# Attention kernel on one core: scores issued for six blocks at a time instead of four

## The chip, the cores and the metric

The kernel runs on one core of one Trainium2 chip. The metric is the device time of one execution in microseconds. Three runs of the kernel before took 1965.5, 1963.23 and 1964.68 us; the median is 1964.68 us.

## The reference

Two attention layers over the same input are mixed by a gate. Layer A has 32 query heads over one shared key and value head, layer B 32 full heads; a head has 16 columns, and there are 2048 tokens.

```python
def _A_ref(x, wq, wk, wv, wo):
    B, S, D = x.shape          # 1, 2048, 512
    H = 32; Dh = D // H        # 16
    q = (x @ wq).reshape(B, S, H, Dh).transpose(0, 2, 1, 3)
    k = x @ wk
    v = x @ wv
    p = softmax(einsum("bhqd,bkd->bhqk", q, k) * (Dh ** -0.5), axis=-1)
    o = einsum("bhqk,bkd->bhqd", p, v)
    return o.transpose(0, 2, 1, 3).reshape(B, S, H * Dh) @ wo
...
g = sigmoid((A_x * gate_w).sum(-1, keepdims=True))
return g * _A_ref(A_x, A_wq, A_wk, A_wv, A_wo) + (1 - g) * _B_ref(A_x, B_wqkv, B_wo)
```

`_B_ref` is the same with keys and values for each head.

## The kernel before

**Blocks.** The work is cut into eight groups of eight heads: a, b, a, b and so on (`groups`), each in two halves of 1024 queries. One *block* is 128 keys against 512 queries of one head, and there are 4096 of them in the list `blocks`. Two neighbouring blocks (two heads, a *pair*) have their scores made by two matmuls side by side on 64 rows each of TensorE (L490, `scores`), into one of three `sc` buffers in PSUM of two banks each. One exp on ScalarE over 128x1024 values (L494) reads the buffer and writes a `pr` buffer in SBUF; there are 2048 exps. Four blocks make a *quad*: its V product (L509, `values`) is four matmuls in f32 side by side on 32 columns each, shown as eight in the profile because each goes over TensorE twice. Sixteen quads add up in one auxiliary bank (`aux0` or `aux1`); then VectorE copies the bank out (`raw`, L514), DMAs sort the rows into `oT` and `dT`, and *norm* tasks (L425 to L432) divide.

**Projections.** Queries and keys of the next half or group, V of the next b group and the output projections are made while the exps run. They are cut into *units*, and a unit into *products* of TensorE (L172, each four matmuls side by side on 32 columns): 12 products for 512 tokens of queries or keys, 12 for four tiles of V, 3 for an output tile. A unit adds up in the auxiliary bank that the V products don't use at the time, and VectorE reads that bank when the unit is done (L333 queries and keys, L385 V, L410 and L412 output). So the next unit's first product waits for that read. The *lays* (L316) then move a finished projection's rows to their places by 32 DMAs from SyncE's queue, eight in each of four lays.

**The order around the change.** The whole order is written out by the program before it runs; each engine then executes its own list in order. One *step* is four blocks: `scores` for two pairs, `values` for the quad of two steps earlier, and `_Tasks.step`. This planner looks at the units still open and at their due steps, works out how many products a step are needed, and issues up to two; a unit's first product comes at the earliest a step after the last unit's end (`rest`). It also takes one side task (a norm, a weight's statistics) a step, and one lay every third step. `left` is the number of steps until the auxiliary banks change roles; a unit is opened only if it can end by then.

The main loop, and what the planner does in it, is in the functions printed here with the line numbers of the profile.

Of the kernel before, what the change touches and what calls it, by code (L numbers as in the profile page):

```python
# [23 lines left out]
NT = S // P  # L24
# [1 line left out]
NG = 4  # L26
BLK = 512
ACT = 2
STEP = 4
COLS = 32  # L30
SCALE = DH ** -0.5

# [3 lines left out]
UP = 2048.0  # L36
# [25 lines left out]
class _Tasks:  # L62
# [1 line left out]


    def __init__(self):
        self.now, self.credit, self.rest = 0, 0.0, 0
        self.units, self.open, self.side = [], deque(), deque()
        self.moves, self.moved = deque(), 0

    def add(self, units, after, due):
        self.units += [(after, due, u) for u in units]
# [8 lines left out]
    def _run(self, left):  # L81
        if not self.open:
            for u in self.units:
                if u[0] <= self.now and self.rest <= self.now and len(u[2]) <= 2 * (left - 1):
                    self.units.remove(u)
                    self.open.extend(u[2])
                    break
        if not self.open:
            return False
        self.open.popleft()()  # L90
        if not self.open:
            self.rest = self.now + 1
        return True

    def step(self, left):
        self.now += 1
        if self.side and self.side[0][0] <= self.now and len(self.open) not in (1, 2):
            self.side.popleft()[1]()
        if self.moves and self.moved <= self.now - 3:
            self.moved = self.now  # L100
            self.moves.popleft()()
        n = len(self.open)
        rate = n / max(1, left - 1)
        for u in self.units:
            n += len(u[2]) + 1
            rate = max(rate, n / max(1, u[1] - self.now))
        self.credit = min(self.credit + rate, 2.2)
        while self.credit >= 1.0 and self._run(left):
            self.credit -= 1.0

    def finish(self):
        while self.open:
            self.open.popleft()()
        self.rest = self.now + 1

    def flush(self):

        assert not self.moves
        self.rest = 0
        ahead = 0  # L120
        while self.open or self.units or self.side:
            if self.side and ahead < 2 and not (self.units and not ahead):
                self.side.popleft()[1]()
                ahead += 1
                continue
            ahead -= ahead > 0
            self.now += 100
            self._run(1 << 20)
            self.finish()
            self.rest = 0  # L130


def _sigmoid(nc, gate, z, scale):
# [8 lines left out]
def _fast(ctx, tc, x, wq_a, wk_a, wv_a, wo_a, wqkv_b, wo_b, gate_w, out, flag):  # L142
    nc = tc.nc
    cst = ctx.enter_context(tc.tile_pool(name="cst", bufs=1))
    inp = ctx.enter_context(tc.tile_pool(name="inp", bufs=8))
    wts = ctx.enter_context(tc.tile_pool(name="wts", bufs=2))
    ops = ctx.enter_context(tc.tile_pool(name="ops", bufs=2))
    prob = ctx.enter_context(tc.tile_pool(name="prob", bufs=6))
    ps_s = ctx.enter_context(tc.tile_pool(name="ps_s", bufs=3, space=PSUM))
    ps_x = ctx.enter_context(tc.tile_pool(name="ps_x", bufs=1, space=PSUM))  # L150

# [11 lines left out]
    vB = cst.tile([P, NT, 4, 3, DH], F32, name="vB")  # L163
# [31 lines left out]
    def load_w(src, gi, queues=(nc.sync, nc.sync)):  # L195

        cols = slice(gi * P, (gi + 1) * P)
        halves = []

        def one(part, at, bufs):  # L200
            w = inp.tile([P, BLK], F32, tag="in", name=f"w{part}{src}{gi}")
            w3 = w.rearrange("p (c m) -> p c m", c=NK)
            queues[part == "o"].dma_start(w if part == "o" else w3,
                                          at if part == "o" else at.rearrange("(c p) m -> p c m", p=P))
            w16 = wts.tile([P, 2, BLK], F16, tag=f"w{part}", name=f"w16{part}{src}{gi}", bufs=bufs)
            weights[src, gi, part] = w16

            def halve():
                split_weight(w16[:, 0], w16[:, 1], w)
                ready.add((part, src, gi))  # L210
                todo.add_side([lambda: absmax(f"w{part}_{src}", gi, w)], todo.now + 2)
# [49 lines left out]
    def x_unit(t):  # L261
        return [lambda: x_one(t, aux[1 - turn[0]])]
# [106 lines left out]
    def v_units(gi):  # L369
        w, state = weights["b", gi, "v"], {}  # L370

        def product(t, part):
            assert ("v", "b", gi) in ready
            a, b = PARTS[part]
            if t % 4 == 0 and part == 0:
                state["ps"] = aux[1 - turn[0]].rearrange("p (t a b d) -> p t a b d", t=4, a=4, b=2)
            ps = state["ps"]
            for c in range(NK):
                by_tiles(ps[:, t % 4].rearrange("p a b d -> p (a b d)"),
                         xT[:, a, c, t * P : (t + 1) * P], w[:, b, c * P : (c + 1) * P],  # L380
                         part == 0 and c == 0, part == 2 and c == NK - 1)
            if t % 4 < 3 or part < 2:
                return
            for hh in range(2):
                nc.vector.tensor_scalar(vB[:, t - 3 : t + 1, :, 2 * hh, :], ps[:, :, :, hh, :], UP ** -2, None,  # L385
                                        op0=ALU.mult)
# [5 lines left out]
        return [[lambda t=t, n=n: product(t, n) for t in range(b, b + 4) for n in range(3)]  # L392
                for b in range(0, NT, 4)]

    oT, dT, o16s = {}, {}, {}

# [21 lines left out]
    def norm_task(src, gi, half, t8, last):  # L418
        def norm():
# [13 lines left out]
            todo.add([o_unit(src, gi, 8 * half + t8, o16, last)], todo.now + 4,  # L433
                     todo.now + (32 if last and half else 52))

        return norm

# [31 lines left out]
    todo.add_side([gates], 15)  # L469


    groups = [(src, gi) for gi in range(NG) for src in "ab"]
# [23 lines left out]
    def values(m):  # L496
# [33 lines left out]
        todo.add_side([norm_task(src, gi, half, t8, last) for t8 in done8], todo.now + (3 if last and half else 7))  # L530

    def flag_stats():
        absmax("v_a", 0, vA[:, :, :DH], AX.XY)
# [28 lines left out]
    def begin(n, half):  # L562

        src, gi = groups[n]
        now = todo.now
        start = lambda n, half: (512 * n + 256 * half) // STEP
        sync = (nc.sync,)
        if half == 0:
            todo.add(q_units(src, gi, 1, sync), now if n else 12, start(n, 1) - 11)
        if n == 0 and half == 0:  # L570
            todo.add_side(load_w(*groups[1]), now + 6)
        if n + 2 < len(groups) and half:
            todo.add_side(load_w(*groups[n + 2]), now + 6)
        if n + 1 == len(groups):
            if half:
                todo.add_side([flag_stats], now + 12)
                todo.add_side([flag_reduce], now + 15)
                todo.add_side([flag_check], now + 27)
            return
        nxt = groups[n + 1]  # L580
        due = start(n + 1, 0) - 18
        if half == 0:
            if nxt[0] == "b":
                todo.add(k_units(nxt[1], 0, sync) + k_units(nxt[1], 1, sync), now + 22, due - 45)
                todo.add(v_units(nxt[1]), now + 22, due + 10)
        else:
            todo.add(q_units(*nxt, 0, sync), now + 3, due)

    turn[0] = 1
    steps = len(blocks) // STEP
    for j in range(steps + 2):
        if j < steps:
            if blocks[STEP * j][2:] == (0, 0, 0, 0, 0):
                begin(*blocks[STEP * j][:2])
            for u in range(STEP * j // ACT, STEP * (j + 1) // ACT):
                scores(u)
        if j >= 2:
            values(j - 2)  # L600
        for f in early.get(j, ()):
            f()
        todo.step(-(j - 1) % NT if j >= 2 else NT)
    todo.flush()


# [138 lines left out]
```

## Time and profile before

| what | before |
|---|---|
| median of three runs | 1964.68 us |
| the profiled execution's own time | 1963.35 us |
| its span | 1961.6 us |
| mean granted clock of TensorE | 0.994 |
| TensorE, matmuls busy | 1908.4 us (97%) |
| ScalarE busy | 1906.1 us (97%) |
| VectorE busy | 559.5 us (29%) |
| V products (L509), 8192 matmuls | 546.3 us for a, 545.5 us for b |
| scores (L490), 4096 matmuls | 319.8 us for a, 359.8 us for b |

A group's row on the page gives line, engine, operation, tiles out and in, shape and count, then the busy time, the mean duration of one, and the idle time of the engine just before them with what ended it. A row of the time line gives start in us, duration in us, engine, line, operation and count; neighbours of one kind are merged, and their overlapping durations are merged too, so the time between two starts says more of TensorE than a duration does.

### The profile page before, as it was taken

What the parts mean: (1) busy time and instruction counts of PE and PEld (TensorE: products, weight loads), DVE (VectorE), ACT (ScalarE), POOL (GpSimd) and SP (SyncE); (2) the same over time, 40 slices, a digit from 0 to 9 for tenths busy, and PEclk for the clock granted to TensorE, in tenths of its full rate; (3) what the DMA queues carried; (4) which work ended last, traced back from release to release, by engine and by line L of the source; (5) the groups of instructions that cost most, each with busy time, mean ns of one, the idle gap of its engine ahead of it and who ended that gap; (6) DMA issues with size and microseconds to landing.
All of it is one profiled execution on the core that took longest, in us unless ns stands there. A gap on an engine that the chain in (4) does not pass through costs nothing.

```text
span 1961.6 us, 46364 instructions
## 1 busy us (share of the span) xinstructions
PE 1908.4 (97%) x19472; PEld 517.5 (26%) x19472; DVE 559.5 (29%) x1093; ACT 1906.1 (97%) x2071; POOL 92.7 (5%) x103
## 2 busy tenths in 40 slices
PE   7999999999999999999999999999999999999997
PEld 4222322222222232222222233222222223222221
DVE  4225042141322414123142332412314241241414
ACT  4999999999999999999999999999999999999995
POOL 5001000200000100020000100002000000000000
PEclk8999999999999999999999999999999999999998
DMA  4022100101011110110101210011100111001012
GB/s 142 7 48 50 31 12 15 47 12 33 7 33 47 33 27 7 31 36 11 29 12 31 59 33 14 12 33 28 27 19 17 34 41 32 12 12 28 6 29 82
DMA packets 55416, 59.82 MB, mean 30 GB/s; under 512 B 21440, under 2 KB 29632, under 8 KB 55200
## 3 DMA queue, kind: packets, MB, share of 16 engines
q1 hardware_dynamic: 53984, 55.66, 11.9%
q8 instruction: 155, 2.54, 0.6%
q0 software_dynamic: 528, 0.69, 0.1%
q14 instruction: 61, 0.50, 0.1%
q10 hardware_dynamic: 688, 0.43, 0.1%
HBM read 10.55 MB, written 4.19 MB: 8 GB/s over the span
## 4 chain that ended last, share of the span: by engine, by line
PE 63%; ACT 18%; issue 13%; DVE 5%; SPq 1%; DMA 0%; ACTq 0%; DVEq 0%
PE aux L509 32%; PE sc L490 19%; ACT pr L494 18%; PE aux L172 11%; DVE dTa L425 1%; DVE stats L176 1%; SPq L316 0%; DMA acc<-in_A_x_dram 0%; DVE lob L180 0%; DVE acc L412 0%; DVE xT L247 0%; SPq L525 0%; DVE yb L333 0%; DVE rawb L514 0%; PE aux L275 0%
## 5 line engine op out<-in xcount | busy, mean ns | idle before, releaser
L494 ACT ACTIVATE pr<-sc 128x1024 f32<-128x1024 f32 x2048 | 1895.2, 1261 | 10.5 <-PE sc L490 6.5
L509 PE MATMUL aux<-pr,vA 128*32 128x512 f32 x4096 | 546.3, 605 | 0.0
L509 PE MATMUL aux<-pr,vB 128*32 128x512 f32 x4096 | 545.5, 605 | 0.0
L490 PE MATMUL sc<-Qb,K 64*128 64x512 f16 x2048 | 359.8, 383 | 18.0
L490 PE MATMUL sc<-Qa,kA 64*128 64x512 f16 x2048 | 319.8, 382 | 3.7 <-ACT pr L494 0.2
L490 PEld LDWEIGHTS <-K 64*128 64x128 f16 x2048 | 99.8, 93 | 466.6 <-issue 464.0
L412 DVE SCALAR_TENSOR_TENSOR acc<-aux,gate_up,acc 128x512 f32<-128x512 f32 x112 | 84.0, 750 | 437.4 <-PE aux L172 437.4
L490 PEld LDWEIGHTS <-kA 64*128 64x128 f16 x2048 | 71.0, 94 | 258.4 <-issue 243.9
L509 PEld LDWEIGHTS aux<-pr,vA 128*32 128x32 f32 x4096 | 80.6, 108 | 197.4 <-issue 195.1
L509 PEld LDWEIGHTS aux<-pr,vB 128*32 128x32 f32 x4096 | 80.9, 108 | 128.5 <-issue 122.2
L172 PE MATMUL aux<-w16ob,o16b 128*32 128x512 f16 x768 | 69.2, 392 | 8.3 <-DVE acc L412 6.0
L172 PEld LDWEIGHTS <-xT 128*32 128x32 f16 x3072 | 55.5, 97 | 63.9 <-issue 63.9
L172 PE MATMUL aux<-xT,w16qb 128*32 128x512 f16 x768 | 66.2, 379 | 3.8 <-DVE rawb L514 2.2
L172 PE MATMUL aux<-w16oa,o16a 128*32 128x512 f16 x768 | 68.6, 379 | 0.1
L172 PE MATMUL aux<-xT,w16qa 128*32 128x512 f16 x768 | 65.8, 379 | 1.3 <-DVE ya L333 0.9
L385 DVE TENSOR_SCALAR vB<-aux 128x256 f32<-128x256 f32 x32 | 12.1, 420 | 181.9 <-PE aux L172 181.9
L425 DVE RECIPROCAL dTb<-dTb 128x128 f32<-128x128 f32 x64 | 60.5, 946 | 10.0 <-DMA dTb<-rawb 9.8
L425 DVE RECIPROCAL dTa<-dTa 128x128 f32<-128x128 f32 x64 | 60.5, 945 | 7.9 <-DMA dTa<-rawa 7.9
L172 PE MATMUL aux<-w16vb,xT 128*32 128x128 f16 x3072 | 61.8, 219 | 0.7 <-DVE rawa L514 0.7
L333 DVE TENSOR_SCALAR yk<-aux 128x512 f32<-128x512 f32 x16 | 11.1, 692 | 176.6 <-PE aux L172 176.6
L172 PE MATMUL aux<-xT,w16kb 128*32 128x512 f16 x768 | 60.9, 379 | 0.0
L333 DVE TENSOR_SCALAR ya<-aux 128x512 f32<-128x512 f32 x16 | 11.1, 692 | 170.6 <-PE aux L172 170.6
(119 smaller groups left out, 598.9 us busy)
## 6 DMA issues: line engine op xcount, KB each, us to landing
acc<-in_A_x_dram SPq DMA_DIRECT2D x16, 256.0 KB, 6.0
oTa<-rawa SPq DMA_DIRECT2D x128, 32.0 KB, 1.9
dTa<-rawa SPq DMA_DIRECT2D x128, 32.0 KB, 2.0
K<-hik SPq DMA_DIRECT2D x128, 32.0 KB, 1.9
K<-lok SPq DMA_DIRECT2D x128, 32.0 KB, 1.9
Qb<-hib SPq DMA_DIRECT2D x128, 32.0 KB, 1.9
Qb<-lob SPq DMA_DIRECT2D x128, 32.0 KB, 2.0
out_dram<-acc SPq DMA_DIRECT2D x16, 256.0 KB, 2.1
```

What stands on the lines that cost most here:

```text
L172: nc.tensor.matmul(out[n : n + COLS], lhsT[:, n : n + COLS], rhs, start=start, stop=stop)
L176: nc.vector.tensor_reduce(stats[:, n, i : i + 1], src, axis=axis, op=ALU.max, apply_absolute_value=True)
L333: nc.vector.tensor_scalar(y, state["ps"], UP ** -2, QK_MAX, op0=ALU.mult, op1=ALU.min)
L385: nc.vector.tensor_scalar(vB[:, t - 3 : t + 1, :, 2 * hh, :], ps[:, :, :, hh, :], UP ** -2, None, op0=ALU.mult)
L412: nc.vector.scalar_tensor_tensor(acc[:, t], state["ps"], g, acc[:, t], op0=ALU.mult, op1=ALU.add)
L425: nc.vector.reciprocal(d, d)
L490: nc.tensor.matmul(sc[:, i], k[r, c * P : (c + 1) * P], Q[src, gi, half, p][r, j * BLK : (j + 1) * BLK], start=True, stop=True)
L494: nc.scalar.activation(probs[u][:, :m], sc[:, :m], AF.Exp, scale=SCALE / (UP * UP))
L509: nc.tensor.matmul(o[32 * i : 32 * i + 32, :], v, probs[at // ACT][:, at % ACT], start=c == 0, stop=c == NT - 1)
```

## The change

The unit of the loop becomes a *burst* of six blocks. In a burst the scores of three pairs are issued one behind another, then the quads whose exps belong to earlier bursts: one in odd bursts, two in even ones. The planner no longer works with rates. It has a clock in nanoseconds with a price for each kind of work (product 216, V product 882, the three pairs 863, three exps 2712). Of three exps' time it takes off the scores and the V products, and issues products of units for what is left, ahead of, between and behind the V products; up to 1990 may be carried over. A new unit may open 880 after the last product of the one before. One side task is taken at each quad, one lay at each burst. V units have six products for two tiles instead of twelve for four. `prob` has seven buffers instead of six, `inp` seven instead of eight. All due times are converted from steps to bursts, some with other distances; the early transposes and key blocks are spread over eight bursts instead of eleven steps.

```diff
-STEP = 4
+BURST = 6
+PRODUCT = 216
+VALUES = 882
+SCORES = 863
+EXPS = 2712
+MOST = 1990
+EMPTY = 880
...
-                if u[0] <= self.now and self.rest <= self.now and len(u[2]) <= 2 * (left - 1):
+                if u[0] <= self.now and self.empty <= self.clock and len(u[2]) <= 1.5 * (left - 1):
...
         self.open.popleft()()
+        self.clock += PRODUCT
         if not self.open:
-            self.rest = self.now + 1
+            self.empty = self.clock + EMPTY
         return True

-    def step(self, left):
-        self.now += 1
+    def products(self, room, left):
+
+        if left <= 1:
+            self.finish()
+        while room >= PRODUCT and self._run(left):
+            room -= PRODUCT
+        return room
+
+    def beside(self):
         if self.side and self.side[0][0] <= self.now and len(self.open) not in (1, 2):
             self.side.popleft()[1]()
-        if self.moves and self.moved <= self.now - 3:
-            self.moved = self.now
-            self.moves.popleft()()
-        n = len(self.open)
-        rate = n / max(1, left - 1)
-        for u in self.units:
-            n += len(u[2]) + 1
-            rate = max(rate, n / max(1, u[1] - self.now))
-        self.credit = min(self.credit + rate, 2.2)
-        while self.credit >= 1.0 and self._run(left):
-            self.credit -= 1.0
...
-    inp = ctx.enter_context(tc.tile_pool(name="inp", bufs=8))
+    inp = ctx.enter_context(tc.tile_pool(name="inp", bufs=7))
...
-    prob = ctx.enter_context(tc.tile_pool(name="prob", bufs=6))
+    prob = ctx.enter_context(tc.tile_pool(name="prob", bufs=7))
...
-                nc.vector.tensor_scalar(vB[:, t - 3 : t + 1, :, 2 * hh, :], ps[:, :, :, hh, :], UP ** -2, None,
+                nc.vector.tensor_scalar(vB[:, t - 1 : t + 1, :, 2 * hh, :], ps[:, :2, :, hh, :], UP ** -2, None,
                                         op0=ALU.mult)
...
-    early = {0: p1, 1: t1, 2: x_unit(12), 3: x_unit(13), 4: x_unit(14), 5: p2, 6: t2, 7: x_unit(15), 8: p3, 10: t3}
+    early = {0: (p1, []), 1: (t1, x_unit(12)), 2: (x_unit(13), []), 3: (p2, []), 4: (t2, x_unit(14)),
+             5: (x_unit(15), []), 6: (p3, []), 7: (t3, [])}
...
-    steps = len(blocks) // STEP
-    for j in range(steps + 2):
-        if j < steps:
-            if blocks[STEP * j][2:] == (0, 0, 0, 0, 0):
-                begin(*blocks[STEP * j][:2])
-            for u in range(STEP * j // ACT, STEP * (j + 1) // ACT):
-                scores(u)
-        if j >= 2:
-            values(j - 2)
-        for f in early.get(j, ()):
-            f()
-        todo.step(-(j - 1) % NT if j >= 2 else NT)
+    done = spare = 0
+    for k in range(-(-len(blocks) // BURST) + 1):
+        todays = blocks[BURST * k : BURST * (k + 1)]
+        todo.now += 1
+        todo.clock = max(todo.clock, k * EXPS) + SCORES
+        for u in range(BURST // ACT * k, BURST // ACT * k + len(todays) // ACT):
+            if blocks[ACT * u][2:] == (0, 0, 0, 0, 0):
+                begin(*blocks[ACT * u][:2])
+            scores(u)
+        quads = min(BURST * k, len(blocks)) // 4 - done
+        spare = min(spare + EXPS - SCORES, MOST)
+        room = spare - VALUES * quads
+        front, behind = early.get(k, ((), ()))
+        for f in front:
+            f()
+        for m in range(done, done + quads):
+            room = todo.products(room, -m % NT)
+            values(m)
+            todo.clock += VALUES
+            todo.beside()
+        done += quads
+        spare = max(todo.products(room, -done % NT), 0)
+        for f in behind:
+            f()
+        if todo.moves:
+            todo.moves.popleft()()
     todo.flush()
```

In the lists of instructions below, `sc956` is the buffer use for pair 956, `pr954` the output of exp 954, `aux0` and `aux1` are the auxiliary banks, and `w16ob1` is an output weight. Each pair has two matmuls and each product four; one row of each is shown. TensorE before, in the middle of the kernel, two steps:

```order
L490 MATMUL sc956_11873<-Qb111_10723,K11_7655 128x512 [waits Activation_49]
...
L490 MATMUL sc957_11878<-Qb111_10723,K11_7655 128x512 [waits Activation_49]
...
L509 MATMUL aux0_82<-pr952_11840,vB_91 32x512 x2
L509 MATMUL aux0_82<-pr953_11845,vB_91 32x512 x2
...
L490 MATMUL sc958_11897<-Qb111_10723,K11_7655 128x512 [waits Activation_49]
...
L490 MATMUL sc959_11902<-Qb111_10723,K11_7655 128x512 [waits Activation_49]
...
L509 MATMUL aux0_82<-pr954_11858,vB_91 32x512 x2
L509 MATMUL aux0_82<-pr955_11863,vB_91 32x512 x2
```

TensorE now, at the same place, an odd and an even burst:

```order
L492 MATMUL sc957_11978<-Qb111_10938,K11_7622 128x512 [waits Activation_49]
...
L492 MATMUL sc958_11983<-Qb111_10938,K11_7622 128x512 [waits Activation_49]
...
L492 MATMUL sc959_11988<-Qb111_10938,K11_7622 128x512 [waits Activation_49]
...
L511 MATMUL aux0_82<-pr954_11945,vB_91 32x512 x2
L511 MATMUL aux0_82<-pr955_11950,vB_91 32x512 x2
L492 LDWEIGHTS K12_7660
L492 MATMUL sc960_12002<-Qb112_10983,K12_7660 128x512 [waits Activation_49]
...
L492 MATMUL sc962_12012<-Qb112_10983,K12_7660 128x512 [waits Activation_49]
...
L511 MATMUL aux0_82<-pr956_11955,vB_91 32x512 x2
L511 MATMUL aux0_82<-pr957_11981,vB_91 32x512 x2
L511 MATMUL aux0_82<-pr958_11986,vB_91 32x512 x2
L511 MATMUL aux0_82<-pr959_11991,vB_91 32x512 x2
```

Between two returns to the scores there stood one V product and now there stand one or two. Pair 959 uses the buffer of pair 956, and pair 962 that of pair 959: the last pair of a burst waits for the last exp of the burst before.

The second place is where one output unit ends and the next begins. TensorE before: the last product of a unit, two steps, and the first product of the next unit, which waits for VectorE's read of the bank:

```order
L172 MATMUL aux0_82<-w16ob1_5287,o16b10_11470 32x512
...
L490 MATMUL sc968_12008<-Qb112_10787,K12_7730 128x512 [waits Activation_49]
...
L509 MATMUL aux1_83<-pr964_11961,vB_91 32x512 x2
L509 MATMUL aux1_83<-pr965_11966,vB_91 32x512 x2
...
L490 MATMUL sc970_12022<-Qb112_10787,K12_7730 128x512 [waits Activation_49]
...
L509 MATMUL aux1_83<-pr966_11992,vB_91 32x512 x2
L509 MATMUL aux1_83<-pr967_11997,vB_91 32x512 x2
...
L172 MATMUL aux0_82<-w16ob1_5287,o16b10_11470 32x512 [waits DVE_49]
```

TensorE now, a few microseconds of work further on, in one burst:

```order
L492 MATMUL sc977_12163<-Qb112_10983,K12_7660 128x512 [waits Activation_49]
...
L173 MATMUL aux0_82<-w16ob1_5295,o16b10_11553 32x512
...
L511 MATMUL aux1_83<-pr972_12133,vB_91 32x512 x2
L511 MATMUL aux1_83<-pr973_12138,vB_91 32x512 x2
...
L173 MATMUL aux0_82<-w16ob1_5295,o16b10_11553 32x512 [waits DVE_49]
...
L492 MATMUL sc978_12190<-Qb112_10983,K12_7660 128x512 [waits Activation_49]
```

One V product now stands between the two units where two steps stood.

More of the change, by code (lines that the diff above doesn't have):

```diff
@@ L66, in __init__ @@
     def __init__(self):
-        self.now, self.credit, self.rest = 0, 0.0, 0
+        self.now, self.clock, self.empty = 0, 0, 0
         self.units, self.open, self.side = [], deque(), deque()
-        self.moves, self.moved = deque(), 0
+        self.moves = deque()
     def add(self, units, after, due):
@@ L127, in flush @@
             self.now += 100
+            self.clock += 10 * EMPTY
             self._run(1 << 20)
             self.finish()
-            self.rest = 0
 def _sigmoid(nc, gate, z, scale):
@@ L210, in halve @@
                 ready.add((part, src, gi))
-                todo.add_side([lambda: absmax(f"w{part}_{src}", gi, w)], todo.now + 2)
+                todo.add_side([lambda: absmax(f"w{part}_{src}", gi, w)], todo.now + 1)
             halves.append(halve)
@@ L374, in product @@
             a, b = PARTS[part]
-            if t % 4 == 0 and part == 0:
+            if t % 2 == 0 and part == 0:
                 state["ps"] = aux[1 - turn[0]].rearrange("p (t a b d) -> p t a b d", t=4, a=4, b=2)
@@ L390, in product @@
                     absmax("v_b", 4 * gi + b, vB[:, 4 * b : 4 * b + 4], AX.XYZW)
-        return [[lambda t=t, n=n: product(t, n) for t in range(b, b + 4) for n in range(3)]
-                for b in range(0, NT, 4)]
+        return [[lambda t=t, n=n: product(t, n) for t in range(b, b + 2) for n in range(3)]
+                for b in range(0, NT, 2)]
     oT, dT, o16s = {}, {}, {}
@@ L432, in norm @@
                 nc.vector.tensor_sub(o16[:, 1], o, o16[:, 0])
-            todo.add([o_unit(src, gi, 8 * half + t8, o16, last)], todo.now + 4,
-                     todo.now + (32 if last and half else 52))
+            todo.add([o_unit(src, gi, 8 * half + t8, o16, last)], todo.now + 3,
+                     todo.now + (21 if last and half else 35))
         return norm
@@ L467, in gates @@
         nc.vector.tensor_scalar(gate_up, gate_up, UP ** -2, None, op0=ALU.mult)
-    todo.add_side([gates], 15)
+    todo.add_side([gates], 10)
     groups = [(src, gi) for gi in range(NG) for src in "ab"]
@@ L529, in values @@
             done8 = range(4 * (s - 2), 4 * (s - 1)) if s >= 2 else []
-        todo.add_side([norm_task(src, gi, half, t8, last) for t8 in done8], todo.now + (3 if last and half else 7))
+        todo.add_side([norm_task(src, gi, half, t8, last) for t8 in done8], todo.now + (2 if last and half else 3))
     def flag_stats():
@@ L565, in begin @@
         now = todo.now
-        start = lambda n, half: (512 * n + 256 * half) // STEP
+        start = lambda n, half: (512 * n + 256 * half) // BURST
         sync = (nc.sync,)
         if half == 0:
-            todo.add(q_units(src, gi, 1, sync), now if n else 12, start(n, 1) - 11)
+            todo.add(q_units(src, gi, 1, sync), now if n else 9, start(n, 1) - 8)
         if n == 0 and half == 0:
-            todo.add_side(load_w(*groups[1]), now + 6)
+            todo.add_side(load_w(*groups[1]), now + 4)
@@ L572, in begin @@
         if n + 2 < len(groups) and half:
-            todo.add_side(load_w(*groups[n + 2]), now + 6)
+            todo.add_side(load_w(*groups[n + 2]), now + 4)
         if n + 1 == len(groups):
             if half:
-                todo.add_side([flag_stats], now + 12)
-                todo.add_side([flag_reduce], now + 15)
-                todo.add_side([flag_check], now + 27)
+                todo.add_side([flag_stats], now + 8)
+                todo.add_side([flag_reduce], now + 10)
+                todo.add_side([flag_check], now + 18)
@@ L579, in begin @@
             return
         nxt = groups[n + 1]
-        due = start(n + 1, 0) - 18
+        due = start(n + 1, 0) - 12
         if half == 0:
             if nxt[0] == "b":
-                todo.add(k_units(nxt[1], 0, sync) + k_units(nxt[1], 1, sync), now + 22, due - 45)
-                todo.add(v_units(nxt[1]), now + 22, due + 10)
+                todo.add(k_units(nxt[1], 0, sync) + k_units(nxt[1], 1, sync), now + (3 if n else 10), due - 30)
+                todo.add(v_units(nxt[1]), now + (3 if n else 10), due + 7)
@@ L586, in begin @@
         else:
-            todo.add(q_units(*nxt, 0, sync), now + 3, due)
+            todo.add(q_units(*nxt, 0, sync), now + 2, due)
     turn[0] = 1
-    steps = len(blocks) // STEP
-    for j in range(steps + 2):
-        if j < steps:
-            if blocks[STEP * j][2:] == (0, 0, 0, 0, 0):
-                begin(*blocks[STEP * j][:2])
-            for u in range(STEP * j // ACT, STEP * (j + 1) // ACT):
-                scores(u)
-        if j >= 2:
-            values(j - 2)
-        for f in early.get(j, ()):
-            f()
-        todo.step(-(j - 1) % NT if j >= 2 else NT)
+    done = spare = 0
```

8 lines of the change are left out of this document (3 added, 5 removed).

## The prediction

> **What bounds the kernel now.** I read the page's busy times first, then its groups, then the time line around single exps.
>
> ```profile
> PE 1908.4 (97%) x19472; PEld 517.5 (26%) x19472; DVE 559.5 (29%) x1093; ACT 1906.1 (97%) x2071; POOL 92.7 (5%) x103
> PE 63%; ACT 18%; issue 13%; DVE 5%; SPq 1%; DMA 0%; ACTq 0%; DVEq 0%
> L494 ACT ACTIVATE pr<-sc 128x1024 f32<-128x1024 f32 x2048 | 1895.2, 1261 | 10.5 <-PE sc L490 6.5
> ```
>
> TensorE and ScalarE both look full, and the chain of waits changes between them. So the question is which of the two has slack, and where. ScalarE's own pace must come first. The next two rows come from two windows of the time line with one beginning; the third column of numbers, after the x, is the count of exps merged.
>
> ```profile
> 404.37 17.08 ACT L494 ACTIVATE pr<-sc 128x1024 f32<-128x1024 f32 x18
> 404.37 116.99 ACT L494 ACTIVATE pr<-sc 128x1024 f32<-128x1024 f32 x127
> 28.28 1.04 ACT L494 ACTIVATE pr<-sc 128x1024 f32<-128x1024 f32 x1
> 1924.36 12.52 ACT L494 ACTIVATE pr<-sc 128x1024 f32<-128x1024 f32 x13
> ```
>
> Between the ends of exp 18 and exp 127 lie 99.91 us, so an exp takes **0.917 us** when nothing starves it. The first starts at 28.28 and the last ends at 1924.36 + 12.52 = 1936.88: 1908.6 us for 2048 exps. At full pace they would take 1.02 + 2047 x 0.9167 = 1877.5. So ScalarE loses only **31 us** in the whole kernel, and no version with these exps can gain more than that. Some 8 to 9 us are lost in the first stretch (from 28.28 to 52.72, the tenth step of two and so 18 exps later, by a row quoted further down: 24.4 us instead of 16.5). The other 22 us are lost where TensorE is too full:
>
> ```profile
> 1000.84 0.61 PE L172 MATMUL aux<-xT,w16qa 128*32 128x512 f16 x8
> 1001.39 0.61 PE L490 MATMUL sc<-Qa,kA 64*128 64x512 f16 x4
> 1001.92 1.06 PE L509 MATMUL aux<-pr,vA 128*32 128x512 f32 x8
> 1002.80 0.40 PE L172 MATMUL aux<-xT,w16qa 128*32 128x512 f16 x4
> 1003.14 0.61 PE L490 MATMUL sc<-Qa,kA 64*128 64x512 f16 x4
> 1939.48 0.83 PE L172 MATMUL aux<-w16ob,o16b 128*32 128x512 f16 x12 [0.84 <-DVE acc L412]
> 1940.36 0.75 DVE L412 SCALAR_TENSOR_TENSOR acc<-aux,gate_up,acc 128x512 f32<-128x512 f32 x1 [0.93 <-PE aux L172]
> 1941.16 0.83 PE L172 MATMUL aux<-w16ob,o16b 128*32 128x512 f16 x12 [0.85 <-DVE acc L412]
> ```
>
> Starts count here, since ends overlap. A V product (x8) holds TensorE 1002.80 - 1001.92 = 0.88. A projection product (x4) holds it 0.215: 0.83 for three against 0.40 for one. One product and the way back to the scores take 0.34, so this switch is 0.12. A step of two exps with one product lasts 1.75 (1001.39 to 1003.14), with two 1.97; ScalarE needs 1.83. So steps with two products starve ScalarE, and the rest does not.
>
> **What the change does to TensorE's load.** One switch out of the scores and one back served two exps, and now serve three. Per six exps (two bursts) TensorE has six score pairs, three V products and on average 3.3 projection products: 2 x (0.12 + 2 x 0.21 + 0.32) + 3 x 0.87 + 3.3 x 0.215 = 5.0 us, against 5.50 for the exps. Load is no longer the bound. (0.21 is a pair before another: 0.53 from the first pair to V, less 0.32, below.)
>
> The Trainium skill, "TensorEngine Tiling (Array Packing)", section Key Properties, states that a change of tiling mode drains the engine. The trace agrees (0.12 and about 0.10 beyond the matmuls themselves), and by this rule alone 341 fewer rounds save some 75 us of TensorE and the kernel gets faster; that is the first rival.
>
> **What it does to the order.** The scores tile has three buffers. The third pair of a burst needs the buffer of the exp just ahead of the burst, the last one that ScalarE was given. TensorE executes in order, so everything behind this pair waits for that exp. Then come all V and projection products of the burst, and only behind them the first pair of the next burst. The rows for the links of this chain:
>
> ```profile
> 56.41 1.03 ACT L494 ACTIVATE pr<-sc 128x1024 f32<-128x1024 f32 x1
> 57.49 0.09 PEld L490 LDWEIGHTS <-kA 64*128 64x128 f16 x1 [0.23 <-issue]
> 57.81 0.16 PEld L509 LDWEIGHTS aux<-pr,vA 128*32 128x32 f32 x8 [0.23 <-issue]
> 52.23 0.61 PE L490 MATMUL sc<-Qa,kA 64*128 64x512 f16 x4
> 52.72 1.02 ACT L494 ACTIVATE pr<-sc 128x1024 f32<-128x1024 f32 x1 [0.72 <-PE sc L490]
> ```
>
> An exp ends at 57.44, and the pair that waits for its buffer starts at 57.49: **0.05**. From that pair to the V product: **0.32**. Switch back: **0.12**. From a pair to its exp's start, ScalarE idle: 52.72 - 52.23 = **0.49**. A starved exp until its end: **1.02**. Together 2.00 us, plus W, the products of one burst. The chain starts at the end of the exp before the burst and ends with the first exp of the next burst, four exps later, for which ScalarE needs 4 x 0.917 = 3.67. So a burst starves nothing only if **W is at most 1.67 us**. Each microsecond above that is a loss, carried on two bursts later, because the burst after next waits for this late exp's followers.
>
> The same chain existed before, with one V product inside: W = 0.88 + 0.215 or 0.43, so 0.36 to 0.57 below the limit. Now a burst with two V products has 2 x 0.87 = 1.75 (0.85 to 0.88 each, since the 0.88 holds the switch from the scores) before any projection product. Those bursts are every second one. The listing of the changed order gives, for the 335 pairs of an even and an odd burst (after the first 12), projection products in the even / odd one: 0/5 in 96, 0/0 in 80, 1/4 in 65, 0/4 in 51, 1/1 or 1/2 in 28, 0/1 to 0/3 in 14, 3/0 in one. Excess over 1.67:
> - even, none: 0.08; even, one: 0.295; even, three: 0.72
> - odd, four: 0.88 + 0.86 = 1.74, so 0.07; odd, five: 1.955, so 0.28; fewer: none.
>
> The even bursts alone: 241 x 0.08 + 93 x 0.295 + 0.7 = **47 us**. If every pair costs the larger of its two: 96 x 0.28 + 93 x 0.295 + 145 x 0.08 + 0.7 = **67 us**. The even and the odd chain run side by side and whichever is late holds up the other through ScalarE, so the loss lies between: stepping "the end two bursts on is the later of this end + 3.83 + W and the next end + 2.75" through the list gives about 59. I take **58**.
>
> Evictions. A new unit's first product waits until VectorE has read the auxiliary bank. The rows at 1939.48 to 1941.16 show such units back to back: 1.68 us for three products of 0.645, so 1.03 us from the end of the last product to the next unit. The planner now leaves 0.88, before it left a whole step (1.75). About 195 units run under the exps (46 of queries and keys, 32 of V, some 120 of the output). 0.15 for two thirds of them is 20 us, and more where a norm (four VectorE operations, 1.78 us by the rows below) stands in front; half of it will fall on bursts that have room. Ends: 0, and 195 x 0.15 + 16 halves x 1.8 = 58. I take **20**, near the lower rows.
>
> Start. Three key blocks and four transposed tiles stand in eight bursts instead of eleven steps; the same work on the same engines. Between 5 and 12 us lost; I take 8, as before.
>
> ```profile
> 993.12 0.95 DVE L425 RECIPROCAL dTb<-dTb 128x128 f32<-128x128 f32 x1
> 994.90 0.95 DVE L425 RECIPROCAL dTb<-dTb 128x128 f32<-128x128 f32 x1
> ...
> L385 DVE TENSOR_SCALAR vB<-aux 128x256 f32<-128x256 f32 x32 | 12.1, 420 | 181.9 <-PE aux L172 181.9
> ...
> 31.73 1.22 SPq L316 DMA_DIRECT2D Qa<-hia  x2
> 33.00 1.22 SPq L316 DMA_DIRECT2D Qa<-loa  x2
> ```
>
> From norm to norm VectorE takes 1.78 us; a V unit's read is 0.42; SyncE issues two transfers in 1.27.
>
> Other edits cost nothing I can see. VectorE reads V in 64 pieces instead of 32; a 128x128 piece of this kind isn't in the trace, so it is bounded by nothing and the old 0.42 each, and VectorE is 29% busy; what of it TensorE waits for is in the evictions' bounds. The four lays of a projection now leave one a burst: 8 issues of 0.63 are 5.1 us against 2.75, so SyncE's queue runs up to 10 us behind, covered by due times 8 to 12 bursts (22 to 33 us) ahead; uncovered, scores would wait those 10 us at each of 23 projections. One buffer more for the exps' output, one less for weights: weights are loaded at least half a group (128 exps, some 117 us) ahead, which covers it.
>
> The sum: losses of 58 + 20 + 8 = 86 instead of 31, so +55 us. The profiled execution took 1963.35 us (span 1961.6; the median of the runs is 1.3 above it). 1963.35 + 55 = **2018 us**.
>
> **Rivals.**
> 1. *Faster: the third buffer doesn't matter.* If the third pair came free early enough, the exps would run at 0.917 throughout and only the start would cost: 31 - 8 = 23 us less, 1940 us. For it: TensorE's load, 5.0 against 5.5. Against it: 2.00 + 1.75 exceeds 3.67 with no projection product at all. It decides if the links are 0.3 shorter than my rows, so that W may be 1.97 and one product beside two V products fits; from 0.2 shorter on the kernel would already gain.
> 2. *No change.* Links 0.16 shorter (W up to 1.83) and free evictions: 93 x 0.135 + 96 x 0.125 + 0.6 = 25, with the start 33 instead of 31, so 1965 us. It needs both at once.
> 3. *Slower, but less.* The even chain alone, evictions hidden: 47 + 8 - 31 = +24, 1987 us.
> 4. *Much slower.* Units often meet norms on VectorE: 67 + 58 + 10 - 31 = +104, 2067 us.
>
> The Trainium skill, "Perfetto Trace Analysis", section Optimization Strategy, says that the same gap repeated on the engine that should be saturated can mean too little SBUF or PSUM for the next tile. The runs of before show hardly any such gap on ScalarE (10.5 us); by this page I would expect one at every second burst's first exp, at the forecast's time.
>
> That the change doesn't do what it says can be left out: the listing shows bursts of three pairs and one or two V products.
>
> **How the numbers follow.** Forecast 0.76, rival 3 0.10, rival 4 0.04, rival 2 0.03, rival 1 0.07. A measurement can tell about 0.2% from no change here. So slower 0.90, same 0.03, faster 0.07. The range leaves out rivals 1, 2 and 4 and little of 3: from 1985 (the even chain alone) to 2040 (67 + 35 + 8 - 31 = +79).
>
> **What would show it.** Right: the mean distance of exps rises from 0.932 (1908.6 / 2047) to about 0.959; ScalarE's idle time from 10.5 us to some tens, ended by the score line; the third pair of a burst starts 0.05 after an exp's end; the first exp of a burst starts late, most often behind bursts with two V products and one projection product, or one and five; TensorE waits for VectorE at output units for about 0.15. Wrong: exps at 0.917 from end to end in stretches with projection products, or a starved first exp without a third pair that waited.

## The result, and the profile after

The changed kernel takes 2025.87 us (median of four runs, 2024.77 to 2026.62), the kernel before 1963.95 us (1963.09 to 1965.5): 1.0314 times as long, 95% interval 1.0296 to 1.0332, or +61.9 us. The profiled execution took 2025.17 us at a clock of 0.994 as before; its span is 2023.4 us.

First the page of the changed kernel: busy times, the shares of the chain that ended last, then the groups of exps (L496) and scores (L492). Lines below the change have moved by one or two.

```profile
PE 1872.9 (93%) x19472; PEld 567.3 (28%) x19472; DVE 563.0 (28%) x1125; ACT 1925.3 (95%) x2071; POOL 93.1 (5%) x103
PE 60%; ACT 25%; issue 7%; DVE 6%; DMA 1%; SPq 0%; ACTq 0%; DVEq 0%; POOL 0%
L496 ACT ACTIVATE pr<-sc 128x1024 f32<-128x1024 f32 x2048 | 1914.1, 1038 | 53.2 <-PE sc L492 42.0
L492 PE MATMUL sc<-Qb,K 64*128 64x512 f16 x2048 | 338.0, 381 | 68.6 <-ACT pr L496 66.7
L492 PE MATMUL sc<-Qa,kA 64*128 64x512 f16 x2048 | 322.7, 381 | 37.5 <-ACT pr L496 32.9
```

TensorE has less to do (1872.9 us busy, 1908.4 before) and stands at 93% instead of 97%. Yet ScalarE is idle for 53.2 us instead of 10.5. The two score rows hold the answer: TensorE itself was idle 106 us ahead of scores, and 99.6 of it ended with an exp. So each engine waits for the other. The view of waits says the same (engine and line, what it waited for: us in total, times, longest). The first fence is the changed kernel, the second the kernel before, whose view has no row of scores that wait for an exp among its larger ones.

```profile
PE sc L492 <- ACT pr L496: 99.7, 309, 0.5
ACT pr L496 <- PE sc L492: 42.0, 105, 2.0
PE aux L173 <- DVE acc L413: 10.7, 10, 1.7
```
```profile
PE aux L172 <- DVE acc L412: 6.0, 7, 0.9
ACT pr L494 <- PE sc L490: 6.5, 12, 1.2
```

The first and the last exps of the changed kernel, from two windows of its time line:

```profile
29.45 1.04 ACT L496 ACTIVATE pr<-sc 128x1024 f32<-128x1024 f32 x1
1986.60 13.40 ACT L496 ACTIVATE pr<-sc 128x1024 f32<-128x1024 f32 x14 [1.97 <-PE sc L492]
```

From 29.45 to 1986.60 + 13.40 = 2000.00 are 1970.55 us, 62 more than the 1908.6 before. The whole change of time lies in this stretch: what lies around it is 52.9 us in sum, as before (53.0). At full pace 2048 exps need 1877.5, so 93 us are lost, where 31 were. About 7.5 of them fall on the first 48 exps; in the other 1999 the ends lie 0.9595 apart on average, which is 85.5 us over 0.9167 each.

Here is one turn of the chain, at an even burst with one projection product ahead of its two V products. The first fence has TensorE's rows of the time line, the second ScalarE's.

```profile
408.35 0.39 PE L492 MATMUL sc<-Qb,K 64*128 64x512 f16 x2 [0.52 <-ACT pr L496]
408.67 0.40 PE L173 MATMUL aux<-xT,w16qa 128*32 128x512 f16 x4
408.90 1.89 PE L511 MATMUL aux<-pr,vB 128*32 128x512 f32 x16
410.72 0.39 PE L492 MATMUL sc<-Qb,K 64*128 64x512 f16 x2
```
```profile
409.98 1.07 ACT L496 ACTIVATE pr<-sc 128x1024 f32<-128x1024 f32 x1
411.21 1.02 ACT L496 ACTIVATE pr<-sc 128x1024 f32<-128x1024 f32 x1 [0.17 <-PE sc L492]
```

TensorE stood for 0.52 us ahead of the third pair, until an exp let go of its buffer. Behind it come one product and sixteen matmuls of V, and only at 410.72 the first pair of the next burst: 2.37 us from pair to pair. ScalarE ended its last exp at 409.98 + 1.07 = 411.05 and got the next at 411.21. That one also lasts the full 1.02, with nothing to overlap, so it ends 0.27 late: the gap of 0.17 and 0.10 more. This is why ScalarE's idle time on the page (53.2) says less than the loss (85.5).

Then I went through every burst after the first 16: how many V and projection products it has by the order, and by how much the first exp of the *next* burst ends later than 0.917 after the one ahead of it.

| V / projection products in the burst | bursts | W by the prediction | over 1.67 | median lateness | sum |
|---|---|---|---|---|---|
| 1 / none to 3 | 123 | up to 1.53 | none | 0.00 | 0.1 us |
| 1 / 4 | 115 | 1.74 | 0.07 | 0.05 | 13.8 us |
| 1 / 5 | 95 | 1.955 | 0.28 | 0.24 | 29.9 us |
| 2 / none | 240 | 1.75 | 0.08 | 0.07 | 11.1 us |
| 2 / 1 | 92 | 1.965 | 0.295 | 0.27 | 30.7 us |
| 2 / 3 | 1 | 2.39 | 0.72 | 1.40 | 1.4 us |

Exps at the second and third place of a burst are never late. Of 399 first exps that come over 0.02 late, with 86.8 us together, 371 (83.5 us) follow a burst whose last pair started within 0.07 us of the end of the exp that held its buffer (a *held* pair). Held pairs are the rule here, 550 of these 666 bursts have one, so this count alone proves little. What tells is the work behind them: of 114 bursts with a held pair, one V product and at most three products, only one is followed by a late exp. In the kernel before there were 184 late ones with 23.5 us, and only 2.6 us of that behind a pair that was held.

### The profile page after: what moved, and what is told of

The parts are those of the page before. It is cut to its first block, busy times and chain, and to the rows that moved or that the text cites. A ratio compares the mean times of both kernels' runs of the same rounds, so it can differ in the third digit from the quotient of the medians.

```text
span 2023.4 us, 46408 instructions
## 1 busy us (share of the span) xinstructions
PE 1872.9 (93%) x19472; PEld 567.3 (28%) x19472; DVE 563.0 (28%) x1125; ACT 1925.3 (95%) x2071; POOL 93.1 (5%) x103
## 4 chain that ended last, share of the span: by engine, by line
PE 60%; ACT 25%; issue 7%; DVE 6%; DMA 1%; SPq 0%; ACTq 0%; DVEq 0%; POOL 0%
PE aux L511 27%; ACT pr L496 25%; PE sc L492 21%; PE aux L173 12%; DVE dTb L426 1%; DVE acc L413 1%; DVE dTa L426 1%; DMA acc<-in_A_x_dram 0%; DVE xT L248 0%; DVE oTb L427 0%; DVE o16b L433 0%; DVE oTa L427 0%; DVE stats L177 0%; DVE o16b L432 0%; ACT xT L247 0%
## 5 line engine op out<-in xcount | busy, mean ns | idle before, releaser
L496 ACT ACTIVATE pr<-sc 128x1024 f32<-128x1024 f32 x2048 | 1914.1, 1038 | 53.2 <-PE sc L492 42.0
L511 PE MATMUL aux<-pr,vB 128*32 128x512 f32 x4096 | 508.1, 597 | 0.0
L511 PE MATMUL aux<-pr,vA 128*32 128x512 f32 x4096 | 506.8, 596 | 0.0
L492 PE MATMUL sc<-Qb,K 64*128 64x512 f16 x2048 | 338.0, 381 | 68.6 <-ACT pr L496 66.7
L492 PE MATMUL sc<-Qa,kA 64*128 64x512 f16 x2048 | 322.7, 381 | 37.5 <-ACT pr L496 32.9
L492 PEld LDWEIGHTS <-K 64*128 64x128 f16 x2048 | 101.9, 94 | 456.1 <-issue 418.9
L492 PEld LDWEIGHTS <-kA 64*128 64x128 f16 x2048 | 100.0, 94 | 388.1 <-issue 336.3
L511 PEld LDWEIGHTS aux<-pr,vB 128*32 128x32 f32 x4096 | 108.9, 109 | 172.4 <-issue 148.2
L511 PEld LDWEIGHTS aux<-pr,vA 128*32 128x32 f32 x4096 | 109.0, 109 | 162.8 <-issue 136.7
L516 DVE COPY rawb<-aux 128x512 f32<-128x512 f32 x32 | 22.1, 692 | 343.6 <-PE aux L511 340.0
L426 DVE RECIPROCAL dTb<-dTb 128x128 f32<-128x128 f32 x64 | 60.5, 946 | 11.1 <-DMA dTb<-rawb 11.1
L334 DVE TENSOR_SCALAR yk<-aux 128x512 f32<-128x512 f32 x16 | 11.1, 691 | 185.6 <-PE aux L173 185.6
L386 DVE TENSOR_SCALAR vB<-aux 128x128 f32<-128x128 f32 x64 | 15.6, 286 | 155.7 <-PE aux L173 155.7
L173 PE MATMUL aux<-xT,w16qb 128*32 128x512 f16 x768 | 52.3, 382 | 3.3 <-DVE rawb L516 1.4
```

Of the source, the lines that this page charges most:

```text
L173: nc.tensor.matmul(out[n : n + COLS], lhsT[:, n : n + COLS], rhs, start=start, stop=stop)
L334: nc.vector.tensor_scalar(y, state["ps"], UP ** -2, QK_MAX, op0=ALU.mult, op1=ALU.min)
L386: nc.vector.tensor_scalar(vB[:, t - 1 : t + 1, :, 2 * hh, :], ps[:, :2, :, hh, :], UP ** -2, None, op0=ALU.mult)
L426: nc.vector.reciprocal(d, d)
L492: nc.tensor.matmul(sc[:, i], k[r, c * P : (c + 1) * P], Q[src, gi, half, p][r, j * BLK : (j + 1) * BLK], start=True, stop=True)
L496: nc.scalar.activation(probs[u][:, :m], sc[:, :m], AF.Exp, scale=SCALE / (UP * UP))
```

## The experiments

Theory 1 is the chain of the prediction: the third pair waits for an exp, and the work W behind it is too long. The rivals are that TensorE's load and its switches decide (theory 2; a switch is the way between scores and the other products), or that evictions (VectorE's reads of the auxiliary bank between units) make most of it (theory 3). For the first four the kernel before took 1962.96 us on their chip, 1.0 less than above, so their distances from the changed kernel's 2025.87 are good to about 1 us.

**1. The third pair behind the first V product.** The same products; only the place of the third pair moves, at the cost of one more round out of the scores and back wherever other work follows it.

```diff
         for u in range(BURST // ACT * k, BURST // ACT * k + len(todays) // ACT):
             if blocks[ACT * u][2:] == (0, 0, 0, 0, 0):
                 begin(*blocks[ACT * u][:2])
-            scores(u)
+            if u % 3 < 2 or not k:
+                scores(u)
...
             values(m)
+            if m == done and 3 * k + 2 < len(blocks) // ACT:
+                scores(3 * k + 2)
```

> The third pair of each burst is issued behind the burst's first V product instead of ahead of it; everything else as in the changed kernel. Theory 1 (the chain through the third buffer bounds the kernel): the products between this pair and the next burst fall from at most 1.96 us to at most 1.1 us, below the limit of 1.67, so the third pair hardly ever starves ScalarE any more; but each burst has one more way out of the scores and back (0.22), so TensorE itself becomes the bound in the dense stretches (2 x 0.86 of scores, 2.6 of V, 1.1 of projections and 0.44 for six exps: 5.85 against 5.50). Sum: about 2013 us, some 13 below the changed kernel, and the number of third pairs that start 0.05 us after an exp's end with a starved exp behind them falls to a few tens. Theory 2 (TensorE's own load bounds the changed kernel): 683 more rounds of 0.22 add 150 us, about 2170 us. Theory 3 (evictions bound it): no change within 5 us of 2026.

Measured: 2015.83 us (2015.02 to 2016.71), 1.0271 times before (1.0254 to 1.0288). Its waits, and the shares of its chain:

```profile
ACT pr L496 <- PE sc L492: 53.3, 150, 2.1
PE sc L492 <- ACT pr L496: 46.0, 97, 0.5
```
```profile
PE 73%; ACT 13%; issue 7%; DVE 5%; DMA 1%; SPq 0%; ACTq 0%; DVEq 0%; POOL 0%
```

The trace has 1148 rounds out of the scores and back where the changed kernel has 683: 465 more and not the 683 more of the expectation, because in the other bursts the third pair runs straight into the next burst's scores. At 0.22 each, theory 2 then gives about 2128 us. More switches, and yet 10 us less: load as the only cause falls. Scores now wait for exps half as long (46.0 us for 99.7). But what is left has another look: of 74.0 us of late exps only 9.1 follow a held pair, and the chain runs over TensorE for 73%. In 48.1 of the 74.0 us TensorE's rows show no gap above 0.06 us for more than 5 us ahead of the late exp's burst (19.8 of 87.0 us in the changed kernel). So the wait went, and most of what is lost now falls where TensorE is full; that the additional switches are what fills it is likely, but was not separated.

**2. The same products, but in the bursts with two V products.** Even bursts may take two products, odd ones three, whatever their time; nothing is carried over.

```diff
-        room = spare - VALUES * quads
+        room = (2 if quads > 1 else 3) * PRODUCT
...
-        spare = max(todo.products(room, -done % NT), 0)
+        todo.products(room, -done % NT)
```

> The same bursts and the same products, handed out otherwise: up to two in the bursts with two V products and up to three in those with one, instead of mostly none and four or five. TensorE's load is the same. Theory 1: bursts with two V products and two projection products hold 1.75 + 0.43 = 2.18 us between the third pair and the next burst, 0.51 over the limit; the listing has 218 of them, so 111 us, with 8 for the others and evictions as before: about 2073 us, 47 above the changed kernel. Theory 2 (load): no change, 2026 within 10. Theory 3 (evictions): the same number of units, no change within 10.

Measured: 2077.9 us, 1.0586 (1.0564 to 1.0607). From the page and the waits of this kernel:

```profile
PE 1866.2 (90%) x19472; PEld 553.9 (27%) x19472; DVE 563.3 (27%) x1125; ACT 1922.8 (93%) x2071; POOL 92.5 (4%) x103
```
```profile
PE sc L492 <- ACT pr L496: 166.4, 434, 0.5
ACT pr L496 <- PE sc L492: 108.2, 244, 2.3
```

TensorE executes the same 19472 matmuls and as many switches, and the time rises by 52 us, as theory 1 gave to within 5. 216 bursts with two V and two products (W 2.18, 0.51 over the limit) are followed by exps that come 0.49 late in the median, 119 us of the 138.7 in all; 134.9 of the 138.7 follow a held pair. It is the place of the products that counts, not their number.

**3. A short read of the output bank.** This prices the evictions alone.

```diff
-                nc.vector.tensor_scalar(acc[:, t], state["ps"], g, None, op0=ALU.mult)
+                nc.vector.tensor_scalar(acc[:, t, :P], state["ps"][:, :P], g, None, op0=ALU.mult)
...
-                nc.vector.scalar_tensor_tensor(acc[:, t], state["ps"], g, acc[:, t], op0=ALU.mult, op1=ALU.add)
+                nc.vector.scalar_tensor_tensor(acc[:, t, :P], state["ps"][:, :P], g, acc[:, t, :P],
+                                               op0=ALU.mult, op1=ALU.add)
```

> The order is the changed kernel's, but VectorE reads only 128 of 512 columns of each output product (the other columns of the output keep the input's values, so three quarters of the output projection are left out of the sum). The read takes about 0.25 us instead of 0.75, so an output unit that follows 0.88 us behind another no longer waits. Theory 1 with the small share of evictions that I gave them: 8 to 15 us less, about 2015 us. Theory 3 (evictions of output units are what the change costs): 40 us or more less, below 1986 us. Evictions cost nothing: 2026 within 3.

Measured: 2012.21 us, 1.025 (1.0233 to 1.0267), 13.7 us less than the changed kernel. Its waits (lines one further down):

```profile
PE sc L493 <- ACT pr L497: 102.7, 324, 0.5
ACT pr L497 <- PE sc L493: 36.8, 106, 1.7
PE aux L173 <- DVE acc L413: 4.6, 6, 1.3
```

The short read took 0.35 us. The output evictions are a side cost, as theory 1 had it. The waits of TensorE for them fall from 10.7 to 4.6 us, those of scores for exps stay. The reads of queries, keys and V were not shortened, so this run says nothing of those. About 9 of the 13.7 us lie between exp 48 and the last, 2.4 ahead of the first exp and behind the last, and the rest is that medians are compared here.

**4. The kernel before with two scores buffers.** If the buffer is what links ScalarE back to TensorE, taking one away from the *old* order must expose the same links.

```diff
-    ps_s = ctx.enter_context(tc.tile_pool(name="ps_s", bufs=3, space=PSUM))
+    ps_s = ctx.enter_context(tc.tile_pool(name="ps_s", bufs=2, space=PSUM))
```

> The kernel before, with two score buffers instead of three and nothing else changed. Theory 1, applied to another order: the second pair of a step now waits for an exp three exps ahead of the one it must not starve, so between it and the next step only 2.75 - 2.00 = 0.75 us fit, and the step holds 0.88 + 1.1 x 0.215 = 1.12. 0.37 lost on every second step of 1024: 189 us, in which the 22 us that TensorE's load costs now disappear: about 2131 us. Theory 2 (load alone decides): unchanged load, 1964 within 10. If the links of the chain are 0.1 us off, 2131 moves by 51.

Measured: 2147.5 us, 1.094 (1.0918 to 1.0962). Its waits:

```profile
ACT pr L494 <- PE sc L490: 114.3, 332, 1.1
PE sc L490 <- ACT pr L494: 102.6, 310, 0.5
```

The same pair of rows appears as in the changed kernel, in an order that had neither row of this size. Of its 206.2 us of late exps, 202.6 follow a held pair. The time is 16 us over the forecast; if all of it lay in the links, it would be 0.03 us on 2.00 by the forecast's rate (51 us for each 0.1). No run shows that.

**5. Bursts of three and two pairs.** An attempt at a kernel with W under the limit nearly everywhere: in the one burst of four that has two V products, the first stands ahead of the third pair.

```diff
+PAIRS = (3, 2, 3, 2)
+BEHIND = 4
-EMPTY = 880
+EMPTY = 1050
...
+        quads = max((last - 2) // 2 if n else total // 2, 0) - done
+        cut = n == 3 and quads > 1
...
+        for u in mine[:2] if cut else mine:
+            pair(u)
...
         for m in range(done, done + quads):
...
             values(m)
+            if cut and i == 0:
+                pair(mine[2])
```

> Bursts of three and two pairs in turn, one V product behind the last pair of every burst: in each burst of three that has two V products the first of them stands ahead of the third pair, and at most four projection products stand behind the last pair. A unit opens 1.05 us after the last product of the one before, not 0.88. Nothing is left out. There are 1022 rounds out of the scores and back instead of 683. Theory 1 (the blocked last pair and the work W behind it, W at most 1.67): W is 0.87 to 1.73, above 1.67 in under one burst in ten and by 0.06, so this kernel is faster than the changed one in spite of its extra switches: 1945 (nothing but the start and a few evictions is lost) to 1990 (evictions and units that crowd). Theory 2 (what counts is TensorE's load and the number of switches): 339 more rounds of 0.22 to 0.33 us make it 75 to 110 us slower than the changed kernel, 2100 to 2135; if TensorE's load never is the bound (its sum is about 1800 us by the rows), the time stays at 2026 where three pairs in a row are the trouble as such. Against the kernel before (1963) theory 1 leaves it open: faster only if the evictions hide.

Measured: 1993.05 us (1992.16 to 1994.7), 1.0151 (1.0134 to 1.0168); the kernel before took 1963.66 us here. Exps and waits of this kernel:

```profile
L499 ACT ACTIVATE pr<-sc 128x1024 f32<-128x1024 f32 x2048 | 1912.0, 1103 | 24.2 <-PE sc L495 21.4
```
```profile
PE sc L495 <- ACT pr L499: 34.0, 93, 0.5
ACT pr L499 <- PE sc L495: 21.4, 32, 3.6
```

33 us faster than the changed kernel, with 340 more rounds out of the scores and back (1023 in the trace), so the load theory misses by over 100 us. It is 3 us above the end of theory 1's range, and 30 slower than before. Of its 55.5 us of late exps, 45.4 follow a pair that was not held: as in experiment 1, the chain is mostly gone. In 29.2 of the 55.5 us TensorE's rows show no gap above 0.06 us for more than 5 us ahead of the late exp's burst, so about half is lost where TensorE is too full for a while. So no kernel here beats the one before.

## Why the prediction was right, step by step

**Sign, size and mechanism** held: +55 us forecast, +61.9 measured, 2018 against 2025.87. Exps lie 0.963 apart (1970.55 / 2047) where 0.959 was forecast.

**The limit on W** held, and the distances from pair to pair show it best. By the links, 4 x 0.917 - 0.05 - 0.49 - 1.02 = 2.11 us may lie between a held third pair and the first pair behind it. Where VectorE reads no bank in between, the median distance is 2.16 (one V product, four products), 2.18 (two, none), 2.38 (one, five) and 2.37 (two, one): 0.05, 0.07, 0.27 and 0.26 over, where 0.07, 0.08, 0.28 and 0.295 were forecast. The median lateness of the table agrees with these figures partly by luck, since two effects offset each other in it. A burst whose own first exp was late has that much more room, which is the forecast's rule of the two chains, and a read of the bank adds time. Without a read, bursts of one V product and four products lose 0.00 in the median (54 of them), with a read 0.19 (61); in experiment 3, 101 without a read lose 0.00. So the 13.8 us of that row are nearly all evictions (12.8). Of the third pairs, 558 of 681 started within 0.07 us of an exp's end. The load view of the same profile, 5.0 us of TensorE for 5.5 us of exps, was true on average and beside the point; experiments 2 and 5 show that.

**The sum is 7 us short** (losses of 86 against 93), and the step that was too small is that of the evictions, taken at 20 us. Losses behind the start are 85.5 us against 58 + 20. The price of 0.15 was about right: 101 of the bursts with products are 0.12 to 0.20 longer from pair to pair than others with the same products, 17 us together, and in each a product waits for VectorE. What I gave too little is the dozen bursts in which VectorE had a norm in front of the read, 15 us together. The forecast also counted only reads of units: in 19 of these 113 bursts TensorE waits for the copy of V's own bank (`raw`), 6 us together. One of the dozen, on the time line of the changed kernel:

```profile
292.69 0.94 DVE L426 RECIPROCAL dTa<-dTa 128x128 f32<-128x128 f32 x1
292.82 0.83 PE L173 MATMUL aux<-w16oa,o16a 128*32 128x512 f16 x12
...
293.66 0.29 DVE L427 SCALAR_TENSOR_TENSOR oTa<-oTa,dTa 128x128 f32<-128x128 f32 x1
293.99 0.23 DVE L432 CAST o16a<-oTa 128x128 f16<-128x128 f32 x1
294.25 0.29 DVE L433 TENSOR_TENSOR o16a<-oTa,o16a 128x128 f16<-128x128 f32 x1
...
294.45 0.75 DVE L411 TENSOR_SCALAR acc<-aux,gate_up 128x512 f32<-128x512 f32 x1
295.25 0.40 PE L173 MATMUL aux<-w16oa,o16a 128*32 128x512 f16 x4 [0.81 <-DVE acc L411]
...
295.47 1.90 PE L511 MATMUL aux<-pr,vB 128*32 128x512 f32 x16
...
297.30 0.82 PE L492 MATMUL sc<-Qb,K 64*128 64x512 f16 x6
297.80 3.77 ACT L496 ACTIVATE pr<-sc 128x1024 f32<-128x1024 f32 x4 [0.86 <-PE sc L492]
```

The unit's products end at 293.65, but VectorE is in the four operations of a norm and reads the bank only at 294.45. The next product waits until 295.25 with both V products behind it, and ScalarE stands for 0.86 before its next exp. The 113 bursts together are 32 us longer than plain ones with the same products; experiment 3 takes that to 16. If the chain costs the 59 that stepping through the list gave, 27 us are left for the evictions. Stepping the same rule through the measured distances gives 82 us of the 87 in the table, and 60 without those 32, which bears out the 59. The split is worked out, not measured, since reads of queries, keys and V were not taken away.

**Start**: 8 forecast, about 7.5 lost up to exp 48. The first exp starts 1.2 us later, and the end behind the last exp is 1.3 us shorter.

**The edits costed at nothing** seem to cost little: outside the exps' stretch the sum didn't change, and inside it the chain and the reads give 82 of the 87 us of late exps. None of these edits was run alone.

**Rivals.** The faster one failed on its own condition: links 0.2 to 0.3 shorter than the rows; no change needed 0.16 and free evictions, and had neither. The 1987 of the even chain alone and the 2067 of crowded norms were both in sight: odd bursts lose 43.8 us and even ones 43.2 by the table, and norms do crowd, but in a dozen places instead of many. The range's upper end, +79, would be 2042 and not 2040, which changes nothing here. The first rival had a rule beside it: the Trainium skill, "TensorEngine Tiling (Array Packing)", section Key Properties, has a change of mode drain the engine. The trace agrees in that TensorE's busy time is 35.5 us lower with 341 fewer rounds; but that time was not what set the end. The Trainium skill, "Perfetto Trace Analysis", section Optimization Strategy, says that the same gap repeated on the engine that should be saturated can mean too little PSUM or SBUF for the next tile. The trace agrees as to the gap: 399 first exps of a burst come late, none at another place. Experiment 4 shows the other side, that one buffer less costs the old order 185 us; one more was not tried.

**What would show it.** All 92 bursts of two V products and one product and all 95 of one and five are followed by a late exp, 137 of the 240 with two and none. All signs came but one: the 0.15 at output units does not stand in the view of waits, which has only ten waits of 1.07 us on average there. It shows in the distance from pair to pair.

## What to carry to other kernels

When one engine fills a ring of buffers in bursts and does other work between them, find the issue that waits for the last buffer, and add up everything behind it on the same queue until the next burst: that sum and the links must fit in the consumer's time for as many tiles as there are buffers, plus one. Longer bursts save switches, but they collect the other work into larger pieces behind the held issue, so the piece must be checked, not the average load. And if the excess is small for each burst, it still adds up: mostly 0.05 to 0.45 us, 371 times, it was 4% of this kernel's time.

## What was not expected of the hardware

A V read of 128x128 takes 0.286 us, where 128x256 took 0.420: half the values cost two thirds of the time. The old row stands in the prediction; this is the group in the changed kernel:

```profile
L386 DVE TENSOR_SCALAR vB<-aux 128x128 f32<-128x128 f32 x64 | 15.6, 286 | 155.7 <-PE aux L173 155.7
```

Both bounds that I had put on such a piece, nothing and 0.42, hold.
